# Three small moves around the hand-over from the first MoE to the second: routing products of block 1 in quarters, the first blocks' tables in PSUM, block 0's slots earlier

## The chip, the cores and the metric

One core of one Trainium2 chip runs the whole program. The metric is device microseconds of one execution: the median of several runs. The kernel before takes 1909.39 us (three runs, 1909.04 to 1911.69).

## The reference

Three stages, all float32:

```python
x = attention(q, k, v, w_phi)            # feature-map attention, reshaped to 2304 tokens x 512
# first MoE: every expert on every token, weights by 8 Sinkhorn rounds over softmax-like logits
out = sum_e P[:, e] * (relu(x @ w1[e]) @ w2[e])          # E = 8, D = 512, F = 1024
# second MoE ("moe2"): top-1 routing on normalised rows
logits = (x / |x|) @ (emb / |emb|).T / tau ; idx = argmax(logits)
out[idx == e] = prob[idx] * (relu(x[idx == e] @ w1[e]) @ w2[e])
```

The second MoE needs the first one's finished rows: for every token an expert, a slot in a list sorted by expert, and a gate weight. Its rows are then gathered by expert in blocks of 128 and multiplied with that expert's weights.

## The kernel before, in words

**Tiling and stages.** The 2304 tokens are 3 blocks (0, 1, 2) of 768, and each block is 6 tiles of 128 tokens. The first MoE walks over 48 layers: 16 half-experts times 3 blocks, with a two-level matrix scheme of 7 products per half layer. The running sum of a block lies in SBUF (`acca` for blocks 0 and 1, `accb` for block 2), as quarters: two halves of the 512 columns by two halves of the tokens, each with two chunks of 128 columns. The last three layers are those of the last half-expert on blocks 0, 1, 2; here the profile shows them at about 1497 to 1536, 1536 to 1584 and 1584 to 1629 us. Then the second MoE starts, with 22 gathered blocks of 128 rows.

**Ticks.** A layer of the last group is a generator of 30 steps ("ticks"): ticks 0 to 13 are the first product (`p1_group`, 6 matmuls each), ticks 14 to 29 the second (`p2_plain`, 6 matmuls each). In `p2_plain` the chunk sums of a block are added on DVE (L834) behind ticks 16 and 17 (token half 0, columns 0 to 127 and 128 to 255), 19 and 21 (token half 0, the other columns), 23, 25, 27 and 29 (token half 1). Between ticks the schedule inserts other work: `at_tick(h, i, fn)` emits fn behind tick i of layer h, and every engine's queue keeps this order of emission. The list `tail` near the end of `build` gives the routing its ticks: numbers below 40 are ticks of the layer on block 1, numbers from 40 are (less 40) ticks of the layer on block 2.

**Routing of a block** (`t0` is its first tile: 0, 6 or 12). `route_a` transposes a tile on TensorE, squares and copies it on ACT and stores the rows to DRAM. `route_l` multiplies the tile with the 8 expert embeddings: 4 column chunks times 4 groups of 32 tokens, 16 tiny matmuls of 8 columns, which the profile shows as 32 records, all into the PSUM tile `pl`. `route_b`, `route_o` find the expert (DVE), `route_p` takes a power on POOL, `route_c` counts ranks (7 tiny matmuls, two DVE operations), `route_d` turns ranks into slots (four DVE operations), `route_s`, `route_w` make the gate weight, and `route_i` scatters token number and weight of one tile to DRAM lists with an indirect DMA of POOL.

For block 1 tiles 0 to 2 have all their products behind tick 24 in one go (48 matmuls, 96 records); tiles 3 to 5 have theirs by column chunk behind ticks 25, 27, 29 and tick 1 of the next layer (12 matmuls each), begun by one zero product on `pl`.

**First blocks.** From blocks 0 and 1 alone (1536 tokens) `first_blocks` works out the first 6 of the gathered blocks: counts per expert, their scan, and per block its expert, its offset and a flag (`meta`), all on DVE with small SBUF tiles (`scan`, `blocks_meta`), in steps behind ticks 3, 4, 6, 7 and 22 of the layer on block 2. Behind tick 8 SP reads `meta` into registers, and behind ticks 10 to 16 it issues the first expert's weights. `gather_first` finds the 128 tokens of gathered block 0 without the DRAM lists: 12 comparisons on DVE (L1108, two behind each of ticks 9 to 14), 12 tiny matmuls (L1113) and one indirect gather on POOL (L1119), the last two behind tick 15. SP reads the lists of the next gathered blocks (`load_ids`) from tick 18 on; POOL gathers them from tick 24 on.

**PSUM.** Tag A has 4 banks, B and C one each, D two. `pl` lies in C, block 0's ranks in C, block 1's ranks in B, `gather_first`'s sum in B.

Of the kernel before, what the change touches and what calls it, by code (L numbers as in the profile page):

```python
# [44 lines left out]
def build(tc, a, out):  # L45
# [5 lines left out]
    live = {}  # L51
# [8 lines left out]
    V, A, G, T, SP = nc.vector, nc.scalar, nc.gpsimd, nc.tensor, nc.sync  # L60
# [162 lines left out]
    ones = c0.tile([P, P], F32, name="ones")  # L223
# [5 lines left out]
    onesb = c0.tile([P, P], BF16, name="onesb")  # L229
# [660 lines left out]
    def route_l(t0, i, ks=range(KD)):  # L890
        r = batch(t0)
        if "pl" not in r:
            r["pl"] = psum("C", [P, 6, E])
        split = len(ks) < KD
        if split and i == TPB // 2 and not ks[0]:
            T.matmul(r["pl"][:, i:TPB, :], onesb, ohc[:, 0, :].unsqueeze(1).to_broadcast([P, TPB - i, E]), start=True, stop=False, skip_group_check=True)
        for k in ks:
            for c in range(0, P, 32):
                T.matmul(r["pl"][c:c + 32, i, :], x2c(t0, i, k)[:, c:c + 32], enT[:, k, :], start=(k == 0 and not split), stop=(k == KD - 1), skip_group_check=True)
# [87 lines left out]
    def scan(nb, nm, q=1):
        cum = sm.tile([P, E], F32, tag="cum", name=f"cum{nm}")[0:q]
        V.tensor_tensor_scan(out=cum, data0=ones[0:q, 0:E], data1=nb, initial=0.0, op0=ALU.mult, op1=ALU.add)
        prev = sm.tile([P, E], F32, tag="prev", name=f"prev{nm}")[0:q]  # L990
        V.tensor_tensor(out=prev, in0=cum, in1=nb, op=ALU.subtract)
        return cum, prev

    def blocks_meta(nb, cum, prev, start, b0, b1):
        n = b1 - b0
        q = P if start is None else 1
        io = iob[0:q, 0:n]
        yield
        if start is None:
            ge = sm.tile([P, NEARLY + 4, E], BF16, name="ge0")[:, 0:NEARLY]  # L1000
        else:
            ge, gp = (sm.tile([1, n, E], BF16, name=f"g{q}{b0}") for q in "ep")
        iob_, nb_, cum_ = io.unsqueeze(2).to_broadcast([q, n, E]), nb.unsqueeze(1).to_broadcast([q, n, E]), cum.unsqueeze(1).to_broadcast([q, n, E])
        ei = sm.tile([P, NBLK - NEARLY], F32, tag="ei", name=f"ei{b0}")[0:q, 0:n]
        ri = sm.tile([P, NBLK - NEARLY], F32, tag="ri", name=f"ri{b0}")[0:q, 0:n]
        V.tensor_tensor(out=ge, in0=iob_, in1=cum_, op=ALU.is_ge)
        V.tensor_reduce(out=ei, in_=ge, axis=AX.X, op=ALU.add)
        if start is not None:
            si_ = sm.tile([1, n], F32, name=f"sb{b0}")
            V.tensor_tensor(out=gp, in0=iob_, in1=prev.unsqueeze(1).to_broadcast([1, n, E]), op=ALU.is_ge)  # L1010
            yield
            V.tensor_tensor(out=gp, in0=gp, in1=ge, op=ALU.subtract)
            V.tensor_tensor(out=gp, in0=gp, in1=start.unsqueeze(1).to_broadcast([1, n, E]), op=ALU.mult)
            yield
            V.tensor_reduce(out=si_, in_=gp, axis=AX.X, op=ALU.add)
        V.tensor_tensor(out=ge, in0=ge, in1=nb_, op=ALU.mult)
        yield
        V.tensor_reduce(out=ri, in_=ge, axis=AX.X, op=ALU.add)
        V.tensor_tensor(out=ri, in0=io, in1=ri, op=ALU.subtract)
        if start is not None:  # L1020
            V.tensor_tensor(out=ri, in0=ri, in1=si_, op=ALU.add)
        yield
        V.tensor_scalar(out=ri, in0=ri, scalar1=float(P), scalar2=None, op0=ALU.mult)
        if start is None:
            V.scalar_tensor_tensor(out=live["slots"][:, NF:NF + 1], in0=ei[:, 0:1], scalar=float(REG), in1=ri[:, 0:1], op0=ALU.mult, op1=ALU.add)
        ei, ri = ei[0:1], ri[0:1]
        V.scalar_tensor_tensor(out=meta[:, 0, b0:b1], in0=ei, scalar=float(REG), in1=ri, op0=ALU.mult, op1=ALU.add)
        V.tensor_scalar_min(ebx[:, b0 + 1:b1 + 1], ei, float(E - 1))
        V.tensor_copy(meta[:, 1, b0:b1], ebx[:, b0 + 1:b1 + 1])
        fl = sm.tile([1, NBLK - NEARLY], F32, tag="fl", name=f"fl{b0}")[:, 0:n]  # L1030
        V.tensor_tensor(out=fl, in0=ebx[:, b0 + 1:b1 + 1], in1=ebx[:, b0:b1], op=ALU.not_equal)
        V.scalar_tensor_tensor(out=meta[:, 2, b0:b1], in0=ei, scalar=float(E) - 0.5, in1=fl, op0=ALU.is_le, op1=ALU.mult)

    def first_blocks():
        nb = counts(0, 2, P)
        cum, prev = scan(nb, 0, P)
        yield from blocks_meta(nb, cum, prev, None, 0, NEARLY)
        yield
# [545 lines left out]
```

## Time and profile before

| what | value |
|---|---|
| median of 3 runs | 1909.39 us |
| profiled execution, its own time | 1914.37 us |
| its span, first to last instruction | 1912.6 us |
| TensorE busy, share of the span | 1881.4 us, 98% |
| VectorE (DVE) busy | 1275.5 us, 67% |
| ScalarE (ACT) busy | 860.5 us, 45% |
| GpSimd (POOL) busy | 972.1 us, 51% |
| mean granted TensorE clock | 0.998 of full speed |

A busy share is a mean over stages that have different limits, so the stretch of the last two layers is read by itself below. The start of a matmul is measured, its end is modelled: in back-to-back products the records overlap, and the pitch of the starts is what counts. "Idle before" in square brackets is the time that the engine stood before the instruction, and what ended it; "issue" means that nothing in the profile accounts for it. The profiled execution and the timed runs are different executions.

### The profile page before, as it was taken

How to read it: one execution, taken by the hardware profiler on the slowest of the kernel's cores; microseconds unless marked ns; L12 is line 12 of the kernel's file. 1: busy time of each engine (PE TensorE's matmuls, PEld its weight loads, DVE VectorE, ACT ScalarE, POOL GpSimd, SP SyncE). 2: the span in 40 equal slices, each digit the busy share in tenths (PEclk: the TensorE clock that was granted, in tenths of full speed). 3: DMA queues.
4: the chain of work that ended last, by engine and by line, in shares of the span. 5: the costliest groups of instructions: out<-in, count | busy, mean ns of one | idle time of the engine just before them, and what ended most of it. 6: DMA issues, size and time to landing. Idle time of an engine off the chain costs nothing.

```text
span 1912.6 us, 34766 instructions
## 1 busy us (share of the span) xinstructions
PE 1881.4 (98%) x13649; PEld 1796.8 (94%) x13649; DVE 1275.5 (67%) x1660; ACT 860.5 (45%) x1258; POOL 972.1 (51%) x694
## 2 busy tenths in 40 slices
PE   9999999999999999999999999999999999999998
PEld 8999999999999999999999999999999988888886
DVE  7775565656657557566575575665755646899995
ACT  4674342433333333424233333333242323989885
POOL 0241377847566565747384655656474733422221
PEclk9999999999999999999999999999999999999999
DMA  5474534545362727354454637272635354263961
GB/s 165 148 275 181 222 135 167 172 129 193 108 232 96 255 73 245 108 193 137 163 175 125 203 103 243 85 261 85 222 113 187 128 163 128 63 208 108 337 205 39
DMA packets 125161, 314.47 MB, mean 164 GB/s; under 512 B 23336, under 2 KB 72248, under 8 KB 124994
## 3 DMA queue, kind: packets, MB, share of 16 engines
q1 hardware_dynamic: 120898, 301.69, 47.3%
q0 software_dynamic: 4096, 10.51, 1.7%
q8 instruction: 110, 1.80, 0.4%
q14 instruction: 57, 0.47, 0.1%
HBM read 335.29 MB, written 32.44 MB: 192 GB/s over the span
## 4 chain that ended last, share of the span: by engine, by line
PE 74%; POOL 13%; issue 7%; DVE 3%; ACT 2%; DMA 2%; SPq 0%; POOLq 0%; DVEq 0%; ACTq 0%
PE Q L414 15%; PE Q L415 15%; PE Q L413 15%; POOL hB L461 3%; POOL w1S L333 3%; POOL hT L461 2%; PE psA L1177 2%; POOL w1A L333 2%; PE psA L1178 2%; PE psD L413 2%; PE psA L1176 2%; PE psR L146 2%; PE psD L414 2%; PE psD L415 2%; PE psD L203 2%
## 5 line engine op out<-in xcount | busy, mean ns | idle before, releaser
L477 DVE TENSOR_TENSOR acca<-acca,Q 128x768 f32<-128x768 f32 x196 | 181.5, 949 | 143.7 <-PE Q L415 143.7
L413 PE MATMUL Q<-hT,w2S 128*128 128x384 f32 x504 | 169.4, 336 | 4.1 <-DVE rd L473 4.1
L461 POOL TENSOR_TENSOR hB<-rb,hB 128x768 fp32r<-128x768 f32 x42 | 77.7, 1850 | 181.6 <-ACT hB L458 181.6
L413 PE MATMUL Q<-xT,w1S 128*128 128x384 f32 x504 | 168.4, 334 | 0.9 <-ACT ra L482 0.9
L414 PE MATMUL Q<-hT,w2S 128*128 128x384 f32 x504 | 168.4, 334 | 0.0
L415 PE MATMUL Q<-hT,w2S 128*128 128x384 f32 x504 | 168.4, 334 | 0.0
L415 PE MATMUL Q<-xT,w1S 128*128 128x384 f32 x504 | 168.3, 334 | 0.0
L414 PE MATMUL Q<-xT,w1S 128*128 128x384 f32 x504 | 168.3, 334 | 0.0
L477 DVE TENSOR_TENSOR accb<-accb,Q 128x768 f32<-128x768 f32 x98 | 90.7, 949 | 73.3 <-PE Q L415 73.3
L333 POOL TENSOR_TENSOR w1A<-raw,w1A 128x512 fp32r<-128x512 f32 x48 | 62.8, 1309 | 137.3 <-ACT w1A L332 137.3
L473 DVE TENSOR_TENSOR Q<-Q,ra 128x768 f32<-128x768 f32 x42 | 40.6, 966 | 133.9 <-PE Q L415 133.9
L482 ACT COPY ra<-Q 128x768 f32<-128x768 f32 x42 | 33.7, 802 | 188.2 <-PE Q L415 166.8
L461 POOL TENSOR_TENSOR hT<-ra,hT 128x768 fp32r<-128x768 f32 x42 | 77.5, 1845 | 69.2 <-ACT hT L458 69.2
L415 PE MATMUL Q<-hB,w2A 128*128 128x384 f32 x336 | 112.3, 334 | 0.0
L415 PE MATMUL Q<-xB,w1A 128*128 128x384 f32 x336 | 112.2, 334 | 0.0
L413 PE MATMUL Q<-xB,w1A 128*128 128x384 f32 x336 | 112.2, 334 | 0.0
L414 PE MATMUL Q<-xB,w1A 128*128 128x384 f32 x336 | 112.2, 334 | 0.0
L413 PE MATMUL Q<-hB,w2A 128*128 128x384 f32 x336 | 112.2, 334 | 0.0
L414 PE MATMUL Q<-hB,w2A 128*128 128x384 f32 x336 | 112.2, 334 | 0.0
L461 POOL TENSOR_TENSOR hT<-rd,hT 128x768 fp32r<-128x768 f32 x42 | 77.9, 1855 | 59.6 <-ACT hT L458 59.5
L1150 DVE TENSOR_TENSOR s1l<-rw,s1h 128x1024 fp32r<-128x1024 f32 x88 | 102.5, 1218 | 3.9 <-ACT s1h L1149 2.2
L473 DVE TENSOR_TENSOR Q<-Q,rc 128x768 f32<-128x768 f32 x42 | 40.6, 966 | 93.8 <-PE Q L415 88.1
(455 smaller groups left out, 6126.2 us busy)
## 6 DMA issues: line engine op xcount, KB each, us to landing
xT<-xpd SPq DMA_DIRECT2D x120, 768.0 KB
rw<-in_moe_w SPq DMA_DIRECT2D x176, 512.0 KB
xB<-xpd SPq DMA_DIRECT2D x90, 768.0 KB
raw<-in_moe_w SPq DMA_DIRECT2D x34, 512.0 KB
gate<-gd SPq DMA_DIRECT2D x45, 384.0 KB
rx<-in_moe_w SPq DMA_DIRECT2D x30, 512.0 KB
xpd<-xT SPq DMA_DIRECT2D x12, 768.0 KB
xpd<-xB SPq DMA_DIRECT2D x9, 768.0 KB
```

The source lines that it names most:

```text
L146: T.matmul(hs[h_][:, c * P:(c + 1) * P], r[rs, c * P:(c + 1) * P], wphi[rs, :], start=True, stop=True)
L203: T.matmul(ps[cs, 2 * ci + h_, :], eq[:, sg, h_, ci * P + cs.start:ci * P + cs.stop], kvz[:, h_, sg, o:o + W], start=(sg == 0), stop=(sg = ...
L333: eng.tensor_tensor(out=t[:, 1], in0=r(nm), in1=f32(t[:, 0]), op=ALU.subtract)
L413: T.matmul(bank, w[:, 0, j, k, :], x[:, 0, k, :], start=start and k == 0, stop=False, skip_group_check=True)
L414: T.matmul(bank, w[:, 0, j, k, :], x[:, 1, k, :], start=False, stop=False, skip_group_check=True)
L415: T.matmul(bank, w[:, 1, j, k, :], x[:, 0, k, :], start=False, stop=stop and k == 1, skip_group_check=True)
L461: eng.tensor_tensor(out=hb[nm][:, 1], in0=src, in1=f32(hb[nm][:, 0]), op=ALU.subtract)
L473: V.tensor_tensor(out=out, in0=x, in1=y, op=op)
L477: V.tensor_tensor(out=z, in0=z, in1=ps, op=op)
L1150: V.tensor_tensor(out=lo, in0=r, in1=f32(hi), op=ALU.subtract)
L1176: T.matmul(ps[hf], th[:, k, :], wh[:, cs], start=(k == 0), stop=False)
L1177: T.matmul(ps[hf], tl[:, k, :], wh[:, cs], start=False, stop=False)
```

## The change

It has three parts and some shifted ticks.

1. Tiles 0 to 2 of block 1 get their embedding products by column chunk too: 12 matmuls behind each of ticks 17, 18, 20 and 22, each one tick behind the sum that it reads. The zero product that begins `pl` now covers all six tiles and stands before the first of them.
2. `first_blocks` keeps its counts, scan, comparisons and sums in one PSUM tile (tag B, float32) in place of SBUF tiles (two of them were bfloat16), with one more copy (the counts into PSUM). The offset for `gather_first` is written one step earlier, behind tick 6.
3. Block 0's ranks move from tick 20 to tick 11 and its slots from 22 to 13, both in the first product of the layer; its weights go from 21 and 23 to 20 and 21, and its six scatters from 24 to 28 to ticks 22 to 27. In the layer on block 2 the tiny matmuls and the gather of `gather_first` move from tick 15 to 16, and the last two scatters of block 1 from 16 and 17 to 17 and 18.

```diff
         if "pl" not in r:
             r["pl"] = psum("C", [P, 6, E])
+            if len(ks) < KD:
+                T.matmul(r["pl"], onesb, ohc[:, 0, :].unsqueeze(1).to_broadcast([P, TPB, E]), start=True, stop=False, skip_group_check=True)
         split = len(ks) < KD
-        if split and i == TPB // 2 and not ks[0]:
-            T.matmul(r["pl"][:, i:TPB, :], onesb, ohc[:, 0, :].unsqueeze(1).to_broadcast([P, TPB - i, E]), start=True, stop=False, skip_group_check=True)
...
     def first_blocks():
         nb = counts(0, 2, P)
-        cum, prev = scan(nb, 0, P)
-        yield from blocks_meta(nb, cum, prev, None, 0, NEARLY)
+        tb = psum("B", [P, P])
+        nbp, cum, rp, ei = tb[:, 0:E], tb[:, E:2 * E], tb[:, 16:16 + NEARLY], tb[:, 24:24 + NEARLY]
+        ge = tb[:, 32:32 + NEARLY * E].rearrange("p (n e) -> p n e", e=E)
+        V.tensor_copy(nbp, nb)
+        V.tensor_tensor_scan(out=cum, data0=ones[:, 0:E], data1=nbp, initial=0.0, op0=ALU.mult, op1=ALU.add)
+        prev = sm.tile([P, E], F32, tag="prev", name="prev0")
+        V.tensor_tensor(out=prev, in0=cum, in1=nb, op=ALU.subtract)
+        yield
+        io = iob[:, 0:NEARLY]
+        V.tensor_tensor(out=ge, in0=io..., in1=cum..., op=ALU.is_ge)
+        V.tensor_reduce(out=ei, in_=ge, axis=AX.X, op=ALU.add)
+        V.tensor_tensor(out=ge, in0=ge, in1=nb..., op=ALU.mult)
+        yield
+        V.tensor_reduce(out=rp, in_=ge, axis=AX.X, op=ALU.add)
+        ri = sm.tile([P, NBLK - NEARLY], F32, tag="ri", name="ri0")[:, 0:NEARLY]
+        V.tensor_tensor(out=ri, in0=io, in1=rp, op=ALU.subtract)
+        V.tensor_scalar(out=ri, in0=ri, scalar1=float(P), scalar2=None, op0=ALU.mult)
+        V.scalar_tensor_tensor(out=live["slots"][:, NF:NF + 1], in0=ei[:, 0:1], scalar=float(REG), in1=ri[:, 0:1], op0=ALU.mult, op1=ALU.add)
+        yield
...
-    tail = route_steps(0, (1, 2, 4, 6, 8, 10), (1, 2, 3, 4, 5, 6), b=8, o=9, p=11, c=20, s=21, d=22, w=23, i=(24, 24, 25, 26, 27, 28))
-    tail += [(k, partial(route_l, TPB, i, (j,))) for j, k in enumerate((25, 27, 29, 41)) for i in range(3, TPB)]
-    tail += route_steps(6, (24, 26, 28, 41, 41, 42), (24, 24, 24), p=42, b=41, o=41, c=42, d=42, s=48, w=50, i=(51, 51, 52, 53, 56, 57))
+    tail = route_steps(0, (1, 2, 4, 6, 8, 10), (1, 2, 3, 4, 5, 6), b=8, o=9, p=11, c=11, d=13, s=20, w=21, i=(22, 23, 24, 25, 26, 27))
+    tail += [(k, partial(route_l, TPB, i + 3 * (j // 4), (j % 4,))) for j, k in enumerate((17, 18, 20, 22, 25, 27, 29, 41)) for i in range(3)]
+    tail += route_steps(6, (24, 26, 28, 41, 41, 42), (), p=42, b=41, o=41, c=42, d=42, s=48, w=50, i=(51, 51, 52, 53, 57, 58))
...
-    tail += [(k, partial(next, gf, None)) for k in (23, 49, 50, 51, 52, 53, 54, 55)]
+    tail += [(k, partial(next, gf, None)) for k in (23, 49, 50, 51, 52, 53, 54, 56)]
```

`scan` and `blocks_meta` lose their branches for the first blocks and serve the later ones alone, with the same operations as before.

## Rows read from the trace of the kernel before

**Rows 1.** Windows: busy us (count) per engine, granted clock PEclk, DMA.

```profile
1569.20:1576.70 7.50, 4.57 (x133) 3.50 (x132) 0.47 (x3) 0.22 (x1) 5.25 (x7) 0.98 0.36 60
1576.70:1579.60 2.90, 2.89 (x11) 2.57 (x11) 0.56 (x1) 1.06 (x3) 0.96 (x1) 0.50 0.31 95
...
1599.30:1603.20 3.90, 2.37 (x13) 2.13 (x13) 3.69 (x17) 0.76 (x2) 0.00 (x0) 1.00 0.17 39
...
1606.60:1609.90 3.30, 1.08 (x14) 0.71 (x13) 2.62 (x9) 1.22 (x3) 1.29 (x3) 1.00 1.01 391
1609.90:1614.10 4.20, 4.20 (x16) 4.20 (x17) 1.50 (x5) 3.55 (x4) 3.43 (x4) 0.59 1.09 247
...
1646.00:1851.00 205.00, 204.20 (x1000) 169.77 (x998) 194.54 (x251) 182.21 (x237) 52.74 (x44) 1.00 0.56 191
```

**Rows 2.** Timeline, PE, layer on block 1: start, length, line, count, [idle before].

```profile
1569.22 0.87 PE L899 MATMUL psC<-enT,acca 128*32 128x8 f32 x83
...
1572.20 0.42 PE L413 MATMUL psD<-hB,w2A 128*128 128x384 f32 x1
...
1574.22 0.25 PE L899 MATMUL psC<-enT,acca 128*32 128x8 f32 x4 [0.48 <-issue]
```

**Rows 3.** Timeline, ACT, then DVE: the first results taken behind that stretch.

```profile
1576.48 0.60 ACT L884 ACTIVATE rows6a<-psB 128x512 f32<-128x512 f32 x1 [8.82 <-remote]
...
1578.66 0.56 DVE L834 TENSOR_TENSOR acca<-psD,acca 128x384 f32<-128x384 f32 x1 [8.66 <-remote]
```

**Rows 4.** Timeline, PE: groups of the same tiny products elsewhere.

```profile
206.28 1.00 PE L758 MATMUL psC<-wgs,xq 128*32 128x16 f32 x96
...
1542.71 0.44 PE L899 MATMUL psC<-enT,acca 128*32 128x8 f32 x32
```

**Rows 5.** Timeline, DVE, layer on block 1: sums and slot operations.

```profile
1559.28 0.56 DVE L436 TENSOR_TENSOR hB<-psA,hB 128x384 fp32r<-128x384 f32 x1 [0.54 <-ACT hB L435]
...
1560.82 0.55 DVE L834 TENSOR_TENSOR acca<-psD,acca 128x384 f32<-128x384 f32 x1
...
1564.73 0.23 DVE L937 TENSOR_REDUCE so<-oh 128x8 f32<-128x48 bf16 x1
1564.99 0.17 DVE L938 TENSOR_TENSOR ohc<-ohc,so 128x8 bf16<-128x8 bf16 x1
...
1566.20 0.56 DVE L834 TENSOR_TENSOR acca<-psD,acca 128x384 f32<-128x384 f32 x1 [1.05 <-PE psD L415]
...
1567.31 0.20 DVE L953 TENSOR_TENSOR sl<-psC,ereg 128x48 f32<-128x48 f32 x1
1567.54 0.21 DVE L954 TENSOR_TENSOR sl<-sl,oh 128x48 f32<-128x48 f32 x1
...
1568.28 0.56 DVE L834 TENSOR_TENSOR acca<-psD,acca 128x384 f32<-128x384 f32 x1
```

**Rows 6.** Timeline, DVE, layer on block 2: first tables and their followers.

```profile
1592.87 1.00 DVE L991 TENSOR_TENSOR prev<-cum,nb 128x8 f32<-128x8 f32 x1
...
1597.20 0.45 DVE L1019 TENSOR_TENSOR ri<-iob,ri 128x6 f32<-128x6 f32 x1
...
1597.90 0.87 DVE L1025 SCALAR_TENSOR_TENSOR slots<-ei,ri 128x1 f32<-128x1 f32 x1
...
1600.40 0.55 DVE L569 TENSOR_TENSOR tu<-psA,tu 128x384 f32<-128x384 f32 x1
...
1609.03 0.73 DVE L1108 TENSOR_SCALAR ohs<-ohs,slots 128x128 bf16<-128x128 bf16 x4
```

**Rows 7.** Timeline, POOL, layer on block 2: a low part; the gather for block 1.

```profile
1597.74 1.02 POOL L446 TENSOR_TENSOR hT<-graw,hT 128x384 fp32r<-128x384 f32 x1
...
1626.82 1.02 POOL L1092 DMA_INDIRECT xgs<-x2d,idt  x1 [0.27 <-POOL idt L1090]
```

**Rows 8.** Timeline, PE: a wait in that layer; the next gathered block's transposes.

```profile
1601.00 0.44 PE L413 MATMUL psA<-xT,w1A 128*128 128x384 f32 x1 [1.53 <-DVE tu L569]
...
1636.38 0.66 PE L1158 MATMUL psA<-ident,xgs 128*128 128x128 f32 x4
```

More of the change, by code (lines that the diff above doesn't have):

```diff
@@ L985, in counts, with scan @@
         return nb
[L987 to L990, printed above, removed]
+    def scan(nb, nm):
+        cum = sm.tile([1, E], F32, tag="cum", name=f"cum{nm}")
+        V.tensor_tensor_scan(out=cum, data0=ones[0:1, 0:E], data1=nb, initial=0.0, op0=ALU.mult, op1=ALU.add)
+        prev = sm.tile([1, E], F32, tag="prev", name=f"prev{nm}")
         V.tensor_tensor(out=prev, in0=cum, in1=nb, op=ALU.subtract)
@@ L995, in blocks_meta @@
         n = b1 - b0
-        q = P if start is None else 1
-        io = iob[0:q, 0:n]
+        io = iob[0:1, 0:n]
         yield
[L999 to L1005, printed above, removed]
+        ge, gp = (sm.tile([1, n, E], BF16, name=f"g{q}{b0}") for q in "ep")
+        iob_, nb_, cum_ = io.unsqueeze(2).to_broadcast([1, n, E]), nb.unsqueeze(1).to_broadcast([1, n, E]), cum.unsqueeze(1).to_broadcast([1, n, E])
+        ei = sm.tile([1, NBLK - NEARLY], F32, tag="ei", name=f"ei{b0}")[:, 0:n]
+        ri = sm.tile([1, NBLK - NEARLY], F32, tag="ri", name=f"ri{b0}")[:, 0:n]
         V.tensor_tensor(out=ge, in0=iob_, in1=cum_, op=ALU.is_ge)
         V.tensor_reduce(out=ei, in_=ge, axis=AX.X, op=ALU.add)
[L1008 to L1015, printed above, removed]
+        si_ = sm.tile([1, n], F32, name=f"sb{b0}")
+        V.tensor_tensor(out=gp, in0=iob_, in1=prev.unsqueeze(1).to_broadcast([1, n, E]), op=ALU.is_ge)
+        yield
+        V.tensor_tensor(out=gp, in0=gp, in1=ge, op=ALU.subtract)
+        V.tensor_tensor(out=gp, in0=gp, in1=start.unsqueeze(1).to_broadcast([1, n, E]), op=ALU.mult)
+        yield
+        V.tensor_reduce(out=si_, in_=gp, axis=AX.X, op=ALU.add)
         V.tensor_tensor(out=ge, in0=ge, in1=nb_, op=ALU.mult)
@@ L1019, in blocks_meta @@
         V.tensor_tensor(out=ri, in0=io, in1=ri, op=ALU.subtract)
-        if start is not None:
-            V.tensor_tensor(out=ri, in0=ri, in1=si_, op=ALU.add)
+        V.tensor_tensor(out=ri, in0=ri, in1=si_, op=ALU.add)
         yield
         V.tensor_scalar(out=ri, in0=ri, scalar1=float(P), scalar2=None, op0=ALU.mult)
-        if start is None:
-            V.scalar_tensor_tensor(out=live["slots"][:, NF:NF + 1], in0=ei[:, 0:1], scalar=float(REG), in1=ri[:, 0:1], op0=ALU.mult, op1=ALU.add)
-        ei, ri = ei[0:1], ri[0:1]
         V.scalar_tensor_tensor(out=meta[:, 0, b0:b1], in0=ei, scalar=float(REG), in1=ri, op0=ALU.mult, op1=ALU.add)
@@ L1035, in first_blocks @@
         nb = counts(0, 2, P)
-        cum, prev = scan(nb, 0, P)
-        yield from blocks_meta(nb, cum, prev, None, 0, NEARLY)
+        tb = psum("B", [P, P])
[7 more added lines that the diff above has]
+        io = iob[:, 0:NEARLY]
+        V.tensor_tensor(out=ge, in0=io.unsqueeze(2).to_broadcast([P, NEARLY, E]), in1=cum.unsqueeze(1).to_broadcast([P, NEARLY, E]), op=ALU.is_ge)
+        V.tensor_reduce(out=ei, in_=ge, axis=AX.X, op=ALU.add)
+        V.tensor_tensor(out=ge, in0=ge, in1=nb.unsqueeze(1).to_broadcast([P, NEARLY, E]), op=ALU.mult)
+        yield
+        V.tensor_reduce(out=rp, in_=ge, axis=AX.X, op=ALU.add)
[3 more added lines that the diff above has]
+        V.scalar_tensor_tensor(out=live["slots"][:, NF:NF + 1], in0=ei[:, 0:1], scalar=float(REG), in1=ri[:, 0:1], op0=ALU.mult, op1=ALU.add)
+        yield
+        V.scalar_tensor_tensor(out=meta[:, 0, 0:NEARLY], in0=ei[0:1], scalar=float(REG), in1=ri[0:1], op0=ALU.mult, op1=ALU.add)
+        V.tensor_scalar_min(ebx[:, 1:NEARLY + 1], ei[0:1], float(E - 1))
+        V.tensor_copy(meta[:, 1, 0:NEARLY], ebx[:, 1:NEARLY + 1])
+        fl = sm.tile([1, NBLK - NEARLY], F32, tag="fl", name="fl0")[:, 0:NEARLY]
+        V.tensor_tensor(out=fl, in0=ei[0:1], in1=ebx[:, 0:NEARLY], op=ALU.not_equal)
+        V.scalar_tensor_tensor(out=meta[:, 2, 0:NEARLY], in0=ei[0:1], scalar=float(E) - 0.5, in1=fl, op0=ALU.is_le, op1=ALU.mult)
         yield
```

## The prediction, made before the change was timed

> **What bounds the kernel now.** I read the windows first. From 1646 us on TensorE is busy 204.20 of 205.00 us [rows 1]: the second MoE is bound by TensorE, so whatever the last two layers of the first MoE give up arrives at the end, unless a transfer is late there. In those two layers the windows show two holes [rows 1]. [...] From 1606.6 to 1609.9 it is busy 1.08 of 3.30 us, and the clock is 0.59 as a mean over the next 4.2 us. A third, smaller one is the wait of 1.53 us at 1601.0 for a DVE operation [rows 8]. Then I read the timelines for what ends the waits. In the first hole it is "issue": a burst of 83 tiny products in 0.87 us, then a few at a time with about 0.48 us between [rows 2]. In the other two it is DVE: its addition at 1600.40 [rows 6] ends the wait at 1601.0, and its last four comparisons, 1609.03 plus 0.73 us [rows 6], end the second hole.
>
> A tick of the second product is 1.04 us: two sums that stand two ticks apart start at 1566.20 and 1568.28 and each follows its products [rows 5].
>
> **The first hole: is it in the timed runs?** The work in the 7.5 us: 96 tiny products (1.00 us for such a group, rows 4), 24 more (0.4), four transposes (0.4), six matmuls (1.04) and a zero product (0.1), 2.9 us in all; so 4.6 us are lost. The half clock in 2.9 us loses half of them, 1.45. The hole costs the profiled execution 6.0 us.
>
> Three things speak against a hole of that size in an execution that isn't profiled. The same burst, 96 records in 1.00 us, ran elsewhere with no gap [rows 4]; so the burst alone doesn't do it. In the hole other engines learn late what TensorE has done: the matmuls from 1572.20 on end 1.04 us later, at 1573.3, but DVE adds their sum at 1578.66, and ACT takes the transposes that stand before 1572.20 at 1576.48 [rows 2, 3]. That is 5.3 and over 4 us, with both engines idle and no releaser on this core that the profile knows ("remote"). The completions back up, not the work or its operands. And the profiled execution took 1914.37 us where the median is 1909.39: 4.98 us more, nearly the 6.0 us of the hole. I take the hole to belong mostly to the recording. For it being real: nothing shows that the 4.98 us lie here and not in the attention stage, which has many small matmuls as well.
>
> [...]
>
> **Part 1, quarters.** Each of the four new groups (24 records) has a fixed cost. From 1.00 us for 96 and 0.44 us for 32 [rows 4] it is 0.16 us a group; three more groups make +0.48. The wider zero product replaces one of the same kind: nothing. If the hole is there in timed runs, the burst that precedes it is gone: -6.0. Its bounds are 0 and -6.0.
>
> **Part 3, block 0's slots in the first product.** TensorE's seven rank products only change place. On DVE two operations go behind tick 11 (0.23 and 0.17, so +0.40) and four behind tick 13 (1567.31 to 1568.28, +0.97) [rows 5]. DVE is late there: the low part at 1559.28 waited for ACT, and the sum of tick 16 at 1560.82 has no idle time before it [rows 5]. It moves by 1.37 to 1562.2 and ends at 1562.75. Its quarter is queued on TensorE behind tick 17, which without waits ends at about 1561.65 (the sum of tick 21 starts at 1566.20; less four ticks and the 0.2 of the rank products), and all matmuls of tick 18 are queued behind it. Wait: about 1.1 us. The low part pushed by 0.40 ends at 1560.24, and the fifth matmul of tick 16 (two matmuls and a tick ahead of 1561.65, a little less than that with the waits it already has) wants it at about 1560.1: 0.2 more. The later quarters follow their sums by a full tick, and these have over a microsecond of idle before them (1.05 at 1566.20), so they don't wait. I take +1.3 for the DVE push (bounds 0, if something of this is already waited for, and 1.8, if 1.37 and 0.40 add up). So the layer on block 1 is +1.8 us where there is no hole, and -4.2 where there is one. What leaves ticks 20 to 23 there was hidden in DVE's idle time and gives nothing. The six scatters come a tick or two earlier in POOL's queue, ahead of the index ramps of `gather_first`; POOL waits there, and nothing reads the lists before tick 18 of the next layer: 0.
>
> **Part 2, tables in PSUM.** In the layer on block 2 three DVE operations of the first tables take 1.00, 0.45 and 0.87 us [rows 6] where one of that size takes 0.17 [rows 5]. POOL's low part of 1.02 us at 1597.74 covers the last of them, which ends with it [rows 6, 7]. These three read two SBUF operands; in the change each has one in PSUM. They lose 2.32 - 0.51 = 1.8 us; the extra copy takes 0.2 and 0.1 goes to small things: DVE is 1.5 us earlier. Bounds: 0.7, if the multiplication by 128 that still goes from SBUF to SBUF is caught as the last of them was, and 1.8. An operation with PSUM among its inputs costs no more than one without (0.20 and 0.21 at 1567.31 and 1567.54, rows 5). [...]
>
> The addition at 1600.40 then ends at 1599.45 instead of 1600.95, and TensorE, which could go on at 1599.5, waits no more. From there to the end of the comparisons DVE stays the bound (TensorE waits for its high and low parts), so the 1.5 us remain and don't add up with those waits: -1.5.
>
> **Part 3, the gather a tick later.** DVE's last comparison ends at 1609.76 before and about 1608.3 after. Tick 16 now lies before the tiny matmuls that need it, where it was behind them: -1.04, less 0.3 for a low part that tick 16 wants early: -0.75. The wait shrinks from 2.2 us (3.30 less 1.08) to about 1.2. After the wait of 1.53 us the clock stayed at 1.00 [rows 1], so I take the half clock as gone: (1 - 0.59) x 4.2 = -1.7. Its bounds are 0 and -1.7. The layer on block 2 is -4.0 in all (bounds -1.5 and -4.5).
>
> What is late next? SP's register loads come with the tables, 1.5 us earlier; the weights with them. The scatters of block 1 end a tick later against TensorE, and the lists, then POOL's gather at 1626.82, hang on them. Its rows are used at 1636.38 [rows 7, 8]: 8.5 us of cover after the 1.02 of the issue, against at most 3.5 that TensorE comes nearer. No new wait, and no loss at the end.
>
> **Sum.** Without the hole +1.8 - 4.0 = -2.2. The profiled execution, which has the hole, goes 6.0 further: 1914.37 - 8.2 = 1906.2. The median has 1909.39 - 2.2 = 1907.2 if the hole was only in the profile, and 1901.2 if it was in all executions.
>
> **The rivals.** (a) The hole is real: 1901.2. For it, the tiny products do stop there, and the gap is in the same units as every other; against it, the late completions and the 4.98 us. (b) Slower: the waits take the hole's place. DVE's push holds TensorE at tick 17, in the middle of the hole-free stretch, and that is enough for the half clock, as 2.9 us of it cost 1.45 before; in the other layer the tensor that still goes through SBUF meets POOL and the comparisons end as late as before. 1909.39 + 1.8 + 1.45 = 1912.6; it decides once the sum of tick 16 ends more than 2 us behind tick 17. Against it: after 1.53 us of waiting the clock did not fall. (c) The layers gain what I say, but the second MoE waits for lists or weights and gives it back: 1909.4. Against it, the 8.5 us.
>
> **Chances.** Forecast (hole only in the profile) 0.52; (a) 0.32; (b) 0.08; (c) 0.08. The predicted time is the forecast's, 1907.2, with 1904.8 to 1909.6 for it alone. The range takes in most of (a) and all of (c): 1900.2 to 1910.4; a fifth of (a), (b) and a little of the forecast are left out. A measurement of this kernel tells 0.2%, 3.8 us, from no change. Faster than 1905.6: 0.30 of (a) and 0.12 of the forecast, 0.42. Slower than 1913.2: 0.05, from (b). The same: 0.53.
>
> **What would show it.** Hole: in the changed kernel's profile the four groups of 24 stand without "issue" gaps, DVE and ACT follow TensorE at once, and the profiled execution exceeds the median by well under 4.98 us; if it still exceeds it by 5, the hole was never what separates the two. Part 3: a wait of about 1 us before the group of tick 17, ended by DVE's sum. Part 2: `prev` and the offset near 0.2 us beside POOL's low parts, and no wait of the product at tick 12. The gather: a wait near 1.2 us before its matmuls and a clock of 1.00 behind them. I am wrong if the median falls by over 5 us (the hole was real) or doesn't fall at all.

## The result and the profile after

The changed kernel takes 1926.19 us (median of 6 runs, 1924.89 to 1926.9), the kernel before 1911.03 on the same chip (6 runs, 1909.04 to 1914.06): ratio 1.0078, 95% interval 1.0065 to 1.0091. It is 15.2 us slower where 2.2 less were forecast, and outside the range. The profiled execution took 1924.89 us with a span of 1923.1, 1.3 under its median, while the one of before lay 3.3 above its own.

The page of after, span and TensorE's line:

```profile
span 1923.1 us, 34766 instructions
PE 1898.6 (99%) x13649; PEld 1812.1 (94%) x13649; DVE 1276.2 (66%) x1661; ACT 860.6 (45%) x1258; POOL 975.1 (51%) x694
```

TensorE has the same instructions as before and is busy 17 us longer. Where, the starts of a few groups tell. The view of one line of the code, kernel before: group and count, length in ns (min/median/max), first and last start in us.

```profile
L413 PE MATMUL Q<-xT,w1S x504: 334/334/446, 268.4 to 1485.5; 128*128 128x384 f32 x168
L413 PE MATMUL Q<-hB,w2A x336: 334/334/334, 282.3 to 1502.7; 128*128 128x384 f32 x168
...
L899 PE MATMUL psC<-enT,acca x384: 169/176/215, 1538.7 to 1586.8; 128*32 128x8 f32 x192
...
L1176 PE MATMUL psA<-s1h,xth x176: 387/389/502, 1629.5 to 1892.1; 128*128 128x512 f32 x176
```

The same of after (its L1190 is L1176 of before):

```profile
L413 PE MATMUL Q<-xT,w1S x504: 336/338/443, 267.0 to 1498.3; 128*128 128x384 f32 x168
L413 PE MATMUL Q<-hB,w2A x336: 336/339/343, 280.8 to 1515.6; 128*128 128x384 f32 x168
...
L899 PE MATMUL psC<-enT,acca x384: 175/176/198, 1552.2 to 1596.6; 128*32 128x8 f32 x192
...
L1190 PE MATMUL psA<-s1h,xth x176: 387/392/495, 1637.2 to 1902.4; 128*128 128x512 f32 x176
```

Read the starts as marks on one road. From the first to the last of the 504 products of x tiles with `w1S`, the body of the first MoE, it is 1217.1 us before and 1231.3 after: 14.2 lost where the change edits nothing. From the first routing product of the layer on block 1 to the first product of the second MoE it is 90.8 before and 85.0 after: 5.8 gained, in the layers that the change edits. From there to the end of the span it is 283.1 before, 285.9 after: 2.8 lost. The first mark lies at 1552.2 instead of 1538.7, 13.5 later; 13.5 less 5.8 and plus 2.8 are the 10.5 between the two spans.

What is slow in the body? The groups of the page of after, all of the same form (busy us, mean ns | idle before):

```profile
L413 PE MATMUL Q<-xT,w1S 128*128 128x384 f32 x504 | 171.4, 340 | 0.9 <-ACT ra L482 0.9
...
L414 PE MATMUL Q<-hT,w2S 128*128 128x384 f32 x504 | 169.3, 336 | 0.0
```

The same two before:

```profile
L413 PE MATMUL Q<-xT,w1S 128*128 128x384 f32 x504 | 168.4, 334 | 0.9 <-ACT ra L482 0.9
...
L414 PE MATMUL Q<-hT,w2S 128*128 128x384 f32 x504 | 168.4, 334 | 0.0
```

The idle time in front of them is the same and the granted clock is 1.00 in all windows of the body, so nothing more is waited for: each product is a little longer. A group of twelve products, from its first start to the start of the next group, is the measure; the median over the layers of the body, by product, is 0.1733 us before in every group. After, it is 0.1767 to 0.1768 where the moving operand is an x tile, `hB` or `hT1`. The profile writes `hT` for the four tiles `hT1` to `hT4`; by the order of the code its products can be told apart, and those of `hT2` to `hT4` have 0.1733 to 0.1738. One place of after shows both, the first of twelve products of `hT2`, the first of twelve of `hB` and the first behind them, 2.08 and 2.12 us apart:

```profile
706.94 0.34 PE L413 MATMUL Q<-hT,w2S 128*128 128x384 f32 x1
...
709.02 0.34 PE L413 MATMUL Q<-hB,w2A 128*128 128x384 f32 x1
...
711.14 0.34 PE L413 MATMUL Q<-xB,w1A 128*128 128x384 f32 x1
```

Then the rows that answer to those of before. Windows of after: a part of the layer on block 1, the stretch behind the gather, the gather, the second MoE [rows 1]:

```profile
1575.00:1592.00 17.00, 15.53 (x221) 13.82 (x220) 6.47 (x19) 3.08 (x8) 6.51 (x9) 1.00 0.65 229
1620.00:1625.00 5.00, 5.00 (x23) 5.00 (x22) 3.08 (x4) 2.24 (x3) 4.09 (x4) 0.69 1.15 202
1616.00:1620.00 4.00, 3.04 (x23) 2.34 (x23) 3.20 (x12) 2.07 (x3) 2.13 (x3) 0.96 1.03 403
1646.00:1851.00 205.00, 204.39 (x1020) 167.52 (x1020) 191.95 (x252) 180.64 (x238) 58.55 (x53) 1.00 0.52 179
```

Timelines of after, TensorE, DVE and ACT [rows 2, 3, 5, 6, 8], each row with its start:

```profile
1575.38 1.01 DVE L958 CAST si<-slots 128x6 int32<-128x6 f32 x1
...
1576.90 0.38 PE L899 MATMUL psC<-enT,acca 128*32 128x8 f32 x24 [1.47 <-DVE acca L834]
1578.45 0.38 PE L899 MATMUL psC<-enT,acca 128*32 128x8 f32 x24
...
1586.76 0.60 ACT L884 ACTIVATE rows6a<-psB 128x512 f32<-128x512 f32 x1 [5.12 <-PE psB L883]
...
1602.83 0.17 DVE L1033 TENSOR_TENSOR prev<-psB,nb 128x8 f32<-128x8 f32 x1
...
1606.36 0.16 DVE L1042 TENSOR_TENSOR ri<-iob,psB 128x6 f32<-128x6 f32 x1
...
1606.84 0.16 DVE L1044 SCALAR_TENSOR_TENSOR slots<-psB,ri 128x1 f32<-128x1 f32 x1
...
1607.16 0.74 DVE L1048 CAST meta<-ebx 1x6 int32<-1x6 f32 x1
...
1609.79 0.44 PE L413 MATMUL psA<-xT,w1A 128*128 128x384 f32 x1 [0.64 <-DVE tu L569]
...
1618.12 0.66 PE L1127 MATMUL psB<-ohs 128*128 128x2 bf16 x4 [0.81 <-DVE ohs L1122]
```

Most of the forecast's signs are there: quarters without gaps, ACT released by TensorE and no longer by "remote", a wait before the quarter of tick 17 ended by DVE's sum, `prev`, the offset and the slots at 0.16 to 0.17 us where they had 1.00, 0.45 and 0.87 [rows 6]. The clock behind the gather fell all the same (0.69 over 5 us). The two slow casts, 1.01 and 0.74 us, end within 0.03 us of a low part on POOL:

```profile
1575.37 0.99 POOL L446 TENSOR_TENSOR hT<-graw,hT 128x384 fp32r<-128x384 f32 x1 [3.98 <-ACT hT L445]
...
1606.88 1.00 POOL L446 TENSOR_TENSOR hT<-graw,hT 128x384 fp32r<-128x384 f32 x1
```

### The profile page after: what moved, and what is told of

It is laid out like the page before. It is cut to its first block, busy times and chain, and to the rows that moved or that the text cites. A ratio compares the mean times of both kernels' runs of the same rounds, so it can differ in the third digit from the quotient of the medians.

```text
span 1923.1 us, 34766 instructions
## 1 busy us (share of the span) xinstructions
PE 1898.6 (99%) x13649; PEld 1812.1 (94%) x13649; DVE 1276.2 (66%) x1661; ACT 860.6 (45%) x1258; POOL 975.1 (51%) x694
## 4 chain that ended last, share of the span: by engine, by line
PE 84%; DVE 8%; issue 3%; POOL 2%; ACT 2%; DMA 1%; POOLq 0%; SPq 0%; ACTq 0%; DVEq 0%
PE Q L414 19%; PE Q L413 19%; PE Q L415 19%; DVE Q L473 2%; PE psR L146 2%; PE psD L203 2%; PE psA L1191 2%; PE psA L1192 2%; PE psA L1190 2%; PE psD L413 1%; PE psD L1224 1%; PE psD L1223 1%; PE psD L1225 1%; PE psD L415 1%; PE psD L414 1%
## 5 line engine op out<-in xcount | busy, mean ns | idle before, releaser
L413 PE MATMUL Q<-xT,w1S 128*128 128x384 f32 x504 | 171.4, 340 | 0.9 <-ACT ra L482 0.9
L415 PE MATMUL Q<-xT,w1S 128*128 128x384 f32 x504 | 171.3, 340 | 0.0
L414 PE MATMUL Q<-xT,w1S 128*128 128x384 f32 x504 | 171.3, 340 | 0.0
L413 PE MATMUL Q<-hB,w2A 128*128 128x384 f32 x336 | 114.2, 340 | 0.0
L415 PE MATMUL Q<-xB,w1A 128*128 128x384 f32 x336 | 114.2, 340 | 0.0
L413 PE MATMUL Q<-xB,w1A 128*128 128x384 f32 x336 | 114.2, 340 | 0.0
L414 PE MATMUL Q<-xB,w1A 128*128 128x384 f32 x336 | 114.2, 340 | 0.0
L414 PE MATMUL Q<-hB,w2A 128*128 128x384 f32 x336 | 114.2, 340 | 0.0
L415 PE MATMUL Q<-hB,w2A 128*128 128x384 f32 x336 | 114.1, 340 | 0.0
```

Source lines behind the costliest of these rows:

```text
L413: T.matmul(bank, w[:, 0, j, k, :], x[:, 0, k, :], start=start and k == 0, stop=False, skip_group_check=True)
L414: T.matmul(bank, w[:, 0, j, k, :], x[:, 1, k, :], start=False, stop=False, skip_group_check=True)
L415: T.matmul(bank, w[:, 1, j, k, :], x[:, 0, k, :], start=False, stop=stop and k == 1, skip_group_check=True)
```

## The experiments

**Theory A, addresses.** The old tables had a tile `ge0` of 10 x 8 bf16, 160 bytes in each partition, in the pool of small tiles. The change drops it. Pools on the left side of SBUF are stacked behind that one, so in the compiled program they all move down by 160 bytes: the weights from byte 10720 of a partition to 10560, and with them `hT2` to `hT4` and the sums. The pools on the right side (x tiles from byte 158688, `hB` and `hT1` from 201696) stay. Before, all these starts were equal modulo 512 (480). Rivals: the new instructions themselves, or the weights' own place. `e1` is the changed kernel with a tile put back that nothing uses; `e2` the kernel before with `ge0` put into a tile that is unused anyway; `g1` the changed kernel with the right side 160 bytes lower too, by 160 unused bytes there.

```
e1  in first_blocks, behind the tile prev0:
+        sm.tile([P, 40], F32, name="pad0")
e2  in blocks_meta:
-            ge = sm.tile([P, NEARLY + 4, E], BF16, name="ge0")[:, 0:NEARLY]
+            ge = live["hpad"][:, 0:NEARLY * E // 2].bitcast(BF16).rearrange("p (n e) -> p n e", e=E)
g1  ahead of the other pools:
+    rp0 = top.enter_context(tc.tile_pool(name="rp0", bufs=1, side="right"))
+    rp0.tile([P, 40], F32, name="pad1")
```

> The changed kernel with one unused tile of 160 bytes a partition where the old table ge0 lay, so that every later tile of the left side of SBUF is at its address of before. Theory 1, addresses: the change made the pool of small tiles 160 bytes shorter, the weights moved by 160 bytes and the activations of the right side did not, and products whose two operands no longer lie alike take 340 ns in place of 334. Then the pitch of the mixed layers is as before (334 ns a record, layer on block 1 from about 1537 us), and the kernel takes 1907 us, 2 to 5 under the kernel before. Theory 2, the edits themselves cost it (quarters, PSUM tables, earlier slots, a different order of the queues): the time stays at 1925 and the records at 340 ns.

> The kernel before, all its instructions as they were, but with its table ge0 in an unused tile of another pool, so that the pool of small tiles is 160 bytes shorter and every address is that of the changed kernel. Theory 1, addresses: 1925 us (14 us over the kernel before), L413 to L415 on w1S and xT at 340 ns, on w2S and hT at 336. Theory 2, the edits: 1911, 334 ns.

> The changed kernel, its weights 160 bytes lower than before as they are there, and an unused tile of 160 bytes at the top of the right side, so that activations and hidden values lie 160 bytes lower too. If the distance of the two operands' addresses decides: 334 ns in all products of the mixed layers and 1908 us, as with the padding. If the weights' own address decides: 340 ns and 1925 us.

`e1`: 1907.98 us, ratio to before 0.9965 (0.9951 to 0.9979). `e2`: 1933.32, 1.0092 (1.0075 to 1.0109), with before at 1915.43 on that chip. `g1`: 1907.62, 0.9993 (0.9983 to 1.0002), with before at 1909.16 on another chip. The body of the first MoE in `e1`, `e2`, `g1`, in this order (first and last start):

```profile
L413 PE MATMUL Q<-xT,w1S x504: 334/334/446, 267.8 to 1484.4; 128*128 128x384 f32 x168
```

```profile
L413 PE MATMUL Q<-xT,w1S x504: 336/338/443, 268.6 to 1500.0; 128*128 128x384 f32 x168
```

```profile
L415 PE MATMUL Q<-xT,w1S x504: 334/334/446, 268.0 to 1485.1; 128*128 128x384 f32 x168
```

1216.6, 1231.4 and 1217.1 us. The loss leaves the changed kernel with a tile that nothing reads, and comes into the kernel before with no other change than the place of one tile. And `g1`, whose weights lie where the changed kernel has them, is fast: it isn't the weights' address, it is how they lie to the moving operand. The changed kernel itself says the same: `hT2` to `hT4` moved down with the weights, and their products kept 0.1733 to 0.1738 us, while those of `hT1`, which stayed, went to 0.1767. So two operands that TensorE itself reads cost 14 us or nothing by their distance: the body has 1231.3 us in the changed kernel and 1216.6 in `e1`. Where they meet, in the memory or in the engine, no run shows.

How does the cost go with the distance? `e3`, `e4` and `e5` are the changed kernel with other pads, the weights 128, 32 and 64 bytes below their old place.

```
e3  +        sm.tile([P, 8], F32, name="pad0")
e4  +        sm.tile([P, 32], F32, name="pad0")
e5  +        sm.tile([P, 24], F32, name="pad0")
```

> The changed kernel with 32 bytes of padding: weights 128 bytes below their place of before. Under theory 1 it tells the step in which the operands' addresses must agree: fast (334 ns, about 1907 us) if a multiple of 128 bytes is enough, 340 ns and about 1924 us if more (256 or 512) or an exact distance is wanted. Theory 2: 1925 whatever the padding.

> The changed kernel with 128 bytes of padding: weights 32 bytes below their place of before. Theory 1: if the operands have to agree in a multiple of 32 bytes, 334 ns and about 1907 us; but the changed kernel with its 160 bytes is such a multiple and is slow, so 340 ns and about 1924 us is the likelier. Theory 2: 1925.

> The changed kernel with 96 unused bytes per partition in its pool of small tiles, so that the weights lie 64 bytes below where they lay before, against the x tiles that stay. If the slower pitch belongs to every distance that is not a multiple of 128 but a small one: pitch 0.1736 us and a time near 1913, as at 32 bytes. If it begins between 32 and 128 bytes at 64 or below: 0.1755 to 0.1764 us for the products from xT with w1S (338 to 340 ns in the mean), time 1920 to 1926.

`e3` took 1923.79 us and `e4` 1913.61 (about 1924 was held to be likelier), one run each, on the chip of `e1`; `e5` 1911.78, one run on a third chip (before 1915.96). The same row for `e3`, `e4`, `e5`:

```profile
L413 PE MATMUL Q<-xT,w1S x504: 336/337/449, 267.3 to 1496.4; 128*128 128x384 f32 x168
```

```profile
L413 PE MATMUL Q<-xT,w1S x504: 335/336/445, 268.7 to 1486.3; 128*128 128x384 f32 x168
```

```profile
L413 PE MATMUL Q<-xT,w1S x504: 332/336/442, 267.6 to 1485.8; 128*128 128x384 f32 x168
```

| weights below the moving tile's place by | body (first to last of the 504) | second MoE to the end of the span |
|---|---|---|
| 0 (before, `e1`, `g1`) | 1217.1, 1216.6, 1217.1 | 283.1, 283.2, 283.0 |
| 32 (`e4`) | 1217.6 | 288.4 |
| 64 (`e5`) | 1218.2 | 285.9 |
| 128 (`e3`) | 1229.1 | 287.9 |
| 160 (after, `e2`) | 1231.3, 1231.4 | 285.9, 286.1 |

So the body loses from somewhere between 64 and 128 bytes on; at 64, where one theory had 1920 to 1926 us, it does not. Only five distances were tried. And distance is not the whole account: the products of `hT3` and `hT4`, whose distance never changes, have 0.1738 us at 160 and 0.1754 at 64.

The second MoE, with other tiles, loses about 3 us at every distance but zero: the mean pitch of its 128x512 products is 0.2284 to 0.2285 us at zero and 0.2312 to 0.2319 at the four others. The last column holds more than that, a wait for a low part that is longer in some profiles, at distance zero too: `f1`, `f3` and `i3` below have 285.0 to 285.5 us there. So 32 and 128, whose profiles have that wait at over 1.7 us, are not shown to be worse than 64 and 160.

**The parts, with the addresses kept.** From here on every kernel with the change has the pad of `e1`, and its parts are undone one by one: the quarters (`f1`, which also has the zero product of before), block 0's slots (`f2`, its ranks in the other PSUM bank), the tables in PSUM (`f3`, the old `scan` and `blocks_meta`, whose `ge0` takes the pad's place).

```
f1  -    tail += [(k, partial(route_l, TPB, i + 3 * (j // 4), (j % 4,))) for j, k in enumerate((17, 18, 20, 22, 25, 27, 29, 41)) for i in range(3)]
    -    tail += route_steps(6, (24, 26, 28, 41, 41, 42), (), ...
    +    tail += [(k, partial(route_l, TPB, i, (j,))) for j, k in enumerate((25, 27, 29, 41)) for i in range(3, TPB)]
    +    tail += route_steps(6, (24, 26, 28, 41, 41, 42), (24, 24, 24), ...
f2  -    tail = route_steps(0, ..., c=11, d=13, s=20, w=21, i=(22, 23, 24, 25, 26, 27))
    +    tail = route_steps(0, ..., c=20, s=21, d=22, w=23, i=(24, 24, 25, 26, 27, 28))
f3  +        cum, prev = scan(nb, 0, P)
    +        yield from blocks_meta(nb, cum, prev, None, 0, NEARLY)
```

> The padded changed kernel with part 1 undone: the products of tiles 0 to 2 again in one go behind tick 24. If the quarters are what brings the padded kernel 7 us under the kernel before: the gaps called issue come back, TensorE idle some 3 us and half clock behind it, 4 to 6 us over the padded kernel, about 1913 where that takes 1908. If the earlier slots and scatters were what removed the hole: no gaps, and within 1 us of the padded kernel, less the wait of 0.6 us at tick 17 that goes.

> The padded changed kernel with the ticks of block 0's ranks, slots, weights and scatters as before (20 to 28), its ranks in bank B since C now holds the quarters' sums. Theory: DVE's sum of tick 16 comes 1.4 us earlier, the wait of 0.6 us behind tick 17 goes, the layer on block 1 is 0.6 us shorter. Rival: the later scatters meet the quarters' bursts and gaps called issue appear, over 1 us longer.

> The changed kernel with part 2 undone: the first tables in SBUF as in the kernel before, ge0 among them, which also puts all addresses back. Theory: the three operations take 1.00, 0.45 and 0.87 us again, TensorE waits 1.5 us at tick 12 of the layer on block 2, and the start of the second MoE comes 1 us later than in the padded kernel (that is what DVE's addition of tick 9 gained there), so 1909 against 1908. If the tables in PSUM gave nothing: the same start.

On the chip of `g1` (before 1909.16, 25 runs): `f1` 1907.84, ratio 0.999 (0.998 to 1.0); `f3` 1909.05, 0.9994 (0.9985 to 1.0004); `f2` 1906.87, one run. All within 1.5 us of `g1`'s 1907.62, so no part shows a value of its own there. `f1` surprised: it has the burst of 96 back, and its timeline shows the burst whole and no gap behind it.

```profile
1569.64 1.10 PE L899 MATMUL psC<-enT,acca 128*32 128x8 f32 x96
```

**The hole.** On one chip the padded change gains 7.4 us on before (`e1`), on another 1.5 (`g1`): the 8.2 and 2.2 that the forecast had with the hole and without it. Before took 1915.43 there and 1909.16 here, with a median granted clock of 0.9965 and 0.998 in its timed executions. Theory: the hole is real on some chips. `h0` is the kernel before, profiled again; `h1` loads the next layer's gate weights, and `h2` issues block 0's scatters, behind the burst and not beside it.

```
h1  -            at_tick(h, 20, partial(load_gate, HS[h + 1][0] // 2, nxt))
    +            at_tick(h, 29 if h == NH - 2 else 20, partial(load_gate, HS[h + 1][0] // 2, nxt))
h2  -    tail = route_steps(0, ..., i=(24, 24, 25, 26, 27, 28))
    +    tail = route_steps(0, ..., i=(28, 28, 29, 29, 29, 29))
```

> The kernel before once more, for a second profile of it. If the gaps marked issue in the layer on block 1 belong to some executions and not to others, this execution's span and its gaps go together: a span near 1907 us and at most 0.5 us of gaps, or a span near 1913 us and 2.5 us or more of gaps with a granted clock under 0.6 in the 3 us behind them. If the gaps are in every execution, they are here too whatever the span.

> The kernel before with the gate weights of the last layer loaded at tick 29 of the layer on block 1 and not at tick 20. Theory that this load's transfers, in flight when the 96 tiny products issue, cause the gaps: no gaps, the layer on block 1 lasts 42.5 to 43.5 us from its first sums' products (47.8 in the first profile of before), and the time is 3 us or more under the kernel before wherever that has gaps. Rival, that the block's scatters cause them or nothing on this core does: gaps as before, time within 1 us of the kernel before.

> The kernel before with block 0's six scatters issued at ticks 28 and 29, behind the 96 tiny products, and not at ticks 24 to 28 beside them. Theory that the burst stalls only where the first scatters issue with it: no gaps, the layer on block 1 lasts 42.5 to 43.5 us, the time 3 us or more under the kernel before wherever that has gaps. Rival, that the burst or the gate load alone does it: the gaps stay, the time is within 1 us of the kernel before.

On this third chip before takes 1915.96 (19 runs), `h1` 1915.93 (ratio 1.0002, 0.9992 to 1.0012), `h2` 1915.48 (1.0003, 0.9993 to 1.0012), `h0` 1916.47 in one run with a span of 1914.6. Timelines of `h0`, TensorE, ACT, DVE:

```profile
1569.48 0.87 PE L899 MATMUL psC<-enT,acca 128*32 128x8 f32 x82
...
1570.79 0.27 PE L899 MATMUL psC<-enT,acca 128*32 128x8 f32 x6 [0.43 <-issue]
...
1571.53 0.28 PE L899 MATMUL psC<-enT,acca 128*32 128x8 f32 x8 [0.47 <-issue]
...
1578.11 0.60 ACT L884 ACTIVATE rows6a<-psB 128x512 f32<-128x512 f32 x1 [10.18 <-issue]
...
1578.88 0.56 DVE L834 TENSOR_TENSOR acca<-psD,acca 128x384 f32<-128x384 f32 x1 [8.62 <-remote]
```

The hole of [rows 2, 3] again, row by row. In `h1` and `h2` the group of routing products keeps its gaps (last column of this view of groups: idle before, by releaser):

```profile
L899 PE MATMUL psC<-enT,acca 128*32 128x8 f32 x384 | 6.4, 181 | 2.7 <-issue 2.7
```

```profile
L899 PE MATMUL psC<-enT,acca 128*32 128x8 f32 x384 | 6.8, 180 | 3.6 <-issue 3.5
```

So neither of the two transfers beside the burst makes it, and both theories that named one are out. On a fourth chip, where before takes 1916.1 us, the parts were told apart: `f1`, `f2` and `e1` again as `i1`, `i2`, `i3`, and `i4`, in which the gather's last step is back a tick earlier.

```
i4  -    tail += route_steps(6, ..., i=(51, 51, 52, 53, 57, 58))
    +    tail += route_steps(6, ..., i=(51, 51, 52, 53, 56, 57))
    -    tail += [(k, partial(next, gf, None)) for k in (23, 49, 50, 51, 52, 53, 54, 56)]
    +    tail += [(k, partial(next, gf, None)) for k in (23, 49, 50, 51, 52, 53, 54, 55)]
```

> The padded changed kernel with the routing products of block 1 back in one burst of 96 and 24 (part 1 undone), again, on another chip. In three profiles of the kernel before and of two variants of it the burst stalls; in this kernel's one profile, from a chip where the kernel before ran in 1909, it did not. If it is the burst alone that stalls on the slower chips: gaps of 2.5 us or more here and a time 4 to 6 us above the padded changed kernel. If it needs block 0's rank products and slots beside it: no gaps, within 1.5 us of the padded changed kernel.

> The padded changed kernel with block 0's ranks, slots and scatters back at their old ticks (ranks in the other bank), again, timed in rounds. If block 0's slots beside the routing products cause the gaps, with or without the quarters: gaps of 2.5 us or more, 4 to 6 us above the padded changed kernel. If the quarters are enough: no gaps, and 0.5 to 1.5 us under the padded changed kernel, for the wait of 0.6 us at tick 17 and the four slot operations ahead of the sums are gone.

> The padded changed kernel (an unused 160-byte tile keeps all addresses), as the base of this call. If the gaps are the kernel before's own and come and go with the chip: 1907 to 1909 here wherever it runs, while the kernel before has 1909 on one chip and 1915 to 1916 on another, with a mean clock under 0.998 where it is slow.

> The padded changed kernel with the last step of the first gather back at tick 55, and block 1's last scatters at 56 and 57. By the forecast the later tick is worth 0.75 us and the clock behind it: here the wait before the tiny matmuls grows from 0.8 to about 1.8 us, and the time is 0.7 to 1.5 us above the padded changed kernel. If what the layers give up is given back by the second MoE's lists: the scatters a tick earlier bring the lists earlier, and the time is equal or up to 1 us less.

| fourth chip, before 1916.1 (18 runs) | us (runs) | ratio to before |
|---|---|---|
| `i1` burst kept | 1913.43 (1908.4 to 1917.58, 10) | 0.9986 (0.9976 to 0.9995) |
| `i2` slots late | 1908.65 (1906.51 to 1911.7, 5) | 0.9956 (0.9938 to 0.9974) |
| `i3` padded change | 1909.61 (1908.14 to 1913.33, 7) | 0.9966 (0.9954 to 0.9977) |
| `i4` gather a tick earlier | 1908.73 (1907.89 to 1910.42, 5) | 0.9965 (0.9951 to 0.9979) |

Timeline of `i1`, TensorE: the kernel of `f1`, instruction for instruction, now with gaps.

```profile
1569.90 0.68 PE L899 MATMUL psC<-enT,acca 128*32 128x8 f32 x46
1571.09 0.64 PE L899 MATMUL psC<-enT,acca 128*32 128x8 f32 x50 [0.50 <-issue]
...
1573.99 0.24 PE L899 MATMUL psC<-enT,acca 128*32 128x8 f32 x4 [0.60 <-issue]
...
1575.42 0.22 PE L899 MATMUL psC<-enT,acca 128*32 128x8 f32 x3 [1.19 <-issue]
```

In all it has 4.7 us of such gaps; `i2` has none in these products, `i4` 0.5, `i3` 1.0. Over all products of the two layers it is 4.7, 1.8, 0.5 and 1.7 us: a part of the stall falls on other products. It is the burst that stalls most, with block 0's slots late (`h0`) or early (`i1`), and the quarters take most of it away, not all; whether the burst stalls is not in the program alone, since `f1` ran it whole on one chip and `i1` did not on another. The clocks and times of the timed executions move with the hole: before takes 1915.43, 1915.96 and 1916.1 us at a median clock of 0.9965, 0.997 and 0.996 on the chips of `e1`, `h0` and `i1`, and 1909.16 at 0.998 on that of `f1`. No run here shows an execution without a record, so whether the hole belongs to the recording stays open, and so does the mechanism of the stall.

`i4` answers for the gather. Timelines of `i3`, then of `i4`, TensorE, the gather's tiny products and the longest wait of the second MoE:

```profile
1605.25 0.67 PE L1128 MATMUL psB<-ohs 128*128 128x2 bf16 x4 [0.80 <-DVE ohs L1123]
...
1673.62 0.50 PE L1192 MATMUL psA<-s1h,xtl 128*128 128x512 f32 x1 [1.84 <-DVE xtl L1177]
```

```profile
1603.18 0.21 PE L1128 MATMUL psB<-ohs 128*128 128x2 bf16 x2 [1.22 <-DVE ohs L1123]
1604.42 0.67 PE L1128 MATMUL psB<-ohs 128*128 128x2 bf16 x4 [1.03 <-DVE ohs L1123]
...
1671.92 0.50 PE L1192 MATMUL psA<-s1h,xtl 128*128 128x512 f32 x1 [0.91 <-DVE xtl L1177]
```

Back at its old tick the gather waits 2.25 us, as before, and not 0.80; but the second MoE then waits 0.91 for a low part where it waited 1.84, and the two times are not to be told apart. And the windows from 1604 to 1608, of `e1`, then of `i4`:

```profile
1604.00:1608.00 4.00, 4.00 (x17) 3.87 (x17) 2.55 (x7) 3.85 (x5) 3.39 (x3) 0.63 1.04 277
```

```profile
1604.00:1608.00 4.00, 3.58 (x22) 3.38 (x23) 2.41 (x10) 3.76 (x5) 2.71 (x3) 1.00 1.20 311
```

After a wait of 0.80 us the clock fell to 0.63, after 2.25 it stayed at 1.00. In `i3`, the kernel of `e1`, it stayed at 1.00 too. The wait in the second MoE goes with that clock: with the gather at its new tick it was 1.80 to 1.85 us where the clock stayed (`i3`, `f1`, `f3`) and 0.77 to 0.93 where it fell (`e1`, `g1`, `f2`, `i2`); in `i1`, where it stayed but a hole came before it, 0.81. From the first product of the second MoE to the end these three took 285.0 to 285.5 us and those four 283.0 to 283.2. What the clock gives, the wait seems to take back; no run changes one of them alone.

`i2`, `i3` and `i4` beat the kernel before on this chip, and `e1` on the first, by 0.3 to 0.4%; the changed kernel without the pad was timed on neither. Which of these is best, these intervals don't tell.

## Why the prediction was wrong, point by point

**The step that failed is the sum itself:** "Without the hole +1.8 - 4.0 = -2.2" has terms for the two edited layers only and takes everything ahead of 1536 us as unchanged. The instructions there are, their data's place is not. What was missing is 14.2 us in the body and 2.8 in the second MoE, 17 of the 17.4 us by which the forecast missed, from a line of the diff that the prediction read as an operation moved to PSUM and not as 160 bytes taken out from under the weights. No rival had it: (b), slower by DVE's push and the half clock, named 1912.6 for another reason. Without the shift the change is worth -1.5 us on one chip (`g1`, whose interval takes in no change) and -7.4 and -6.5 on two others (`e1`, `i3`).

**Hole.** Given 0.52 to be of the recording only; that was too simple. On the chips where before takes 1915 to 1916 us the profiles of `h0` and `i1` have it, and by their time and clock and the gain of the padded change the timed executions do too; on the one with 1909 most, by time and clock, don't; the chip of the result lies between (1911.03). Rival (a) was right on the former, the forecast on the latter. The argument that 96 such products ran elsewhere without a gap [rows 4] was sound as far as it went, as `f1` shows; it could not speak for other executions. That the quarters take it away held for the most part: in all profiles with them 0 to 1.8 us of "issue" gaps are left in the two layers, against 2.9 to 4.9 in all with the burst but `f1`.

**DVE's push at tick 17.** Forecast about 1.1 us, and 0.2 for the low part: 0.60 in `e1`, 0.61 in `i3`, no second wait. A slip is in it: 1566.20 less four ticks and 0.2 is 1561.84 and not 1561.65, which makes the wait 0.9. In the changed kernel as it stands it is 1.47: there the cast of the slots, ahead of the sum on DVE, took 1.01 us instead of 0.17 and ended with POOL's low part. In `e1` the two start at the same 1560.81 and the cast takes 0.17. With the slots back at their old ticks (`i2`) the time is not to be told from that of `i3`.

**Tables in PSUM.** The three slow operations went to 0.16 or 0.17 us as forecast. But a cast of `meta` that was quick before now takes 0.74 (0.75 in `e1`): coming earlier, it meets a low part on POOL and ends with it (1607.90 and 1607.88), as the slots did before. And the wait of 1.53 [rows 8] shrank to 0.64 and did not vanish: 0.9 where 1.5 was taken. With the tables back (`f3`) the wait is back, and the time is not to be told apart.

**Gather a tick later.** The wait became 0.80 (forecast 1.2), 1.45 less than in `i4`. "No new wait, and no loss at the end" failed: the second MoE's wait for a low part rose from 0.80 before to 1.84 in `i3` (rival (c), in part), though it was 0.82 in `e1`, the same kernel.

**Half clock gone, -1.7.** Failed in after (0.69 over 5 us) and in `e1`, held in `i3` and `i4`. The wait's length didn't decide it, and where it held with the new tick the second MoE mostly gave about 2 us back, so the term should have stood as a bound and not at its full value. With this 1.7, the 0.6 of the tables and 0.4 for the longer wait at tick 17 taken off, and 0.4 for the gather put on, the 8.2 that the profiled pair should have gained in the two layers become 5.9; the marks show 5.8.

## What to carry to other kernels

A tile added to or dropped from a pool moves every pool stacked behind it, here by 160 bytes and at 14.2 us in the body; before costing an edit, compare the addresses of the operands of the busiest products, and pad the pool so that they stay. When a change slows what it doesn't touch, compare the first and last start of a long unchanged group ahead of it, then undo the layout alone. A stall that only one profile shows has to be looked for on more than one chip before it is booked as noise or as gain.

## What the hardware showed that was not expected

- The pitch of a 128x384 product was 0.1733 us with the starts of weights and moving tile equal modulo 512 bytes, and 0.1767 with the weights 160 bytes below: 2% on such a product and 1.2% on a stage bound by TensorE (busy 398.38 of 400 us from 800 us on, before), with no new wait in the profile. Whether another modulus would do, no run tells.
- The same program stalled in a burst of 96 tiny products on one chip (4.7 us of gaps, results taken over 5 us late) and ran it in 1.10 us on another.
- The granted clock behind the same wait of 0.80 us was 0.63 in one execution and 1.00 in another of the same kernel.
- A DVE cast of six numbers in one partition took 0.74 us in the changed kernel and 0.16 before, that of the slots 1.01 and 0.17. When the slow operations of [rows 6] got an input in PSUM, a neighbour of theirs became slow. Both slow casts end within 0.03 us of an operation of POOL.
